# Attention and a gated feed-forward block in one kernel: copies moved between engines, weight decode moved, one pair's sums in other PSUM banks

## The chip, the cores and the metric

One core of a Trainium2 chip runs the whole program. The metric is the device time of one execution in microseconds (us), median of several runs. The engines are TensorE (PE in the profile), VectorE (DVE), ScalarE (ACT), GpSimd (POOL) and SyncE (SP), whose queue issues nearly all DMAs.

## The reference

Attention over 4 batches, 8 heads, 576 positions and 64 channels, with a bias that a small two-layer network makes from the distance of two positions, and then a feed-forward block over the 2304 tokens of 512 channels with 2048 hidden units. All data is fp32.

```python
scores = scale * q @ k.T + bias.transpose(2, 0, 1)[None]
attn = np.exp(scores - np.max(scores, axis=-1, keepdims=True))
attn = attn / (np.sum(attn, axis=-1, keepdims=True) + 1e-09)
x = (attn @ v).transpose(0, 2, 1, 3).reshape(B * S, H * D)
h = x @ w_in
r = np.maximum(h, 0.0)
out = (s * (r * r) + b) @ w_out
```

The weights `w_in` and `w_out` arrive as 64-bit floats, so the kernel loads them as pairs of 32-bit words and puts the fp32 bits together itself ("decode").

## The kernel before, in words

**Stages.** First the bias table is made and stored (about the first 48 us). Then come 16 pairs (a head and two batches), numbered p = 0 to 15. Last comes the feed-forward part, whose first products begin while the last pair ends.

**A pair** has five steps, u = 0 to 4. Step number n = 5p + u issues, in this order: the transposes of the probabilities of unit n on TensorE (`probs_t`, line 349, into the two PSUM tiles named `tps`), the score products of unit n + 2 (`scores`, lines 275 and 282, into `sps`), and the sums over values of the pair before (`av`, lines 438 and 441, into `xps`). VectorE adds the bias to `sps` and takes the row's least value (`biased`, line 297, DVE's custom instruction, writes `tt` and `mn`). ScalarE makes the exponentials (`expo`, line 308, `pr`). The transposed probabilities leave the two `tps` tiles by two copies: the first half on ScalarE (line 377), the second on VectorE (line 379), both into `pt`. There are only two `tps` tiles, so the transposes of the next step wait for both copies. At u = 3 VectorE makes the reciprocal row sums (`norm`, lines 320 and 322), and at u = 4 both engines make four small copies (lines 393 and 395). `tails` (line 398) is one more ScalarE copy at u = 2. When a pair's sums are complete VectorE multiplies them by the reciprocals (lines 444 and 445) into `rb`. The sums lie in one PSUM tile, `xps`, of which there is one buffer.

**Decode in the pairs.** A generator (`early_work`) spreads the decode of the first group of weights over the pairs 1 to 12: eight blocks, each with one step on ScalarE (line 494, absolute value), one on GpSimd (line 496), and three on VectorE (lines 498, 501, 504).

**Feed-forward.** Weights and tokens are cut in 2 x 2 blocks and multiplied by a seven-product scheme: each item n (a group of 512 hidden units and 768 tokens, 12 items) has two halves s, and each half seven products m (`product`, line 638, into `hps`). The operands of a product are sums of blocks (lines 544 and 588), split into a high part (ScalarE, line 597, `x_hi`) and the rest (VectorE, line 601, `x_lo`). The results are combined (lines 660 to 719) into `gt`, and multiplied by `w_out` (`project`, line 754, into `o`).

**What sets the order.** The order of each engine's queue is the order in which the program is written. In the feed-forward part it is a table of slots: slot T issues one product, some projections, and then the events that `at(T, ...)` put there, sorted by a small priority. Slots 0 to 13 hold a product alone, slot 14 six projections and a product; the later slots hold one product each and in every seven slots twelve projections.

**Where the stages meet.** After the last pair's transposes the program runs `prep` for seven operands of the first tokens, two products, starts the decode of two blocks of the second group of `w_in` (`soon_w`, raw tiles `rw`), makes two sums, issues the last `av` of pair 15, and only then the combining of slot 1, whose first step (`keep`, line 660) copies the first product's bank.

```python
for m in FIRST:
    prep(m)
product(0, 0, FIRST[0], False)
product(0, 0, FIRST[1], False)
decs = [decode_w(*e) for e in soon_w]
```

Of the kernel before, what the change touches and what calls it, by code (L numbers as in the profile page):

```python
# [26 lines left out]
def attention_moe(ctx, tc, q, k, v, w_in, w_out, dist, par, out):  # L27
# [310 lines left out]
    def probs_t(n):  # L338
# [79 lines left out]
    late_x = []  # L418
# [6 lines left out]
    def av(p, i, hf):  # L425
# [4 lines left out]
        if i == 0 and hf == 0:  # L430
            accs[p] = ps_x.tile([128, 2, 512], F32, tag="x", name="xps")
        ps = accs[p]
        n = END if hf else CUT
        c = slice(hf * CUT, hf * CUT + n)
        for x in range(2):
            o = ps[64 * x:64 * x + 64, hf, 0:n]
            if kb < 4:
                nc.tensor.matmul(o, vt[:, 4 * x + kb, :], pt[:, kb, x, c], start=(i == 0), stop=(i == 4))  # L438
            else:
                d = slice(64 * (x ^ hf), 64 * (x ^ hf) + 64)  # L440
                nc.tensor.matmul(o, vt[d, 8 + x, :], ptr[d, c], start=False, stop=False)
        if i == 4 and hf == 1:
            xs = rbs.pop(p)
            nc.vector.tensor_tensor(xs[:, 0:CUT], ps[:, 0, 0:CUT], xs[:, 0:CUT], op=ALU.mult)
            nc.vector.tensor_tensor(xs[:, CUT:S], ps[:, 1, 0:n], xs[:, CUT:S], op=ALU.mult)
# [7 lines left out]
    soon_w = []  # L453
# [34 lines left out]
    def decode_w(kind, g, i):  # L488
# [17 lines left out]
        r = w_raw.pop((kind, g, i))  # L506
        if (kind, g, i) not in soon_w:
            free_raw.append(r)
# [483 lines left out]
    def x_make(q, m, free):  # L992
        x_new(q, m)
        for e in range(2):
            x_hi(q, m, e)
        for e in range(2):
# [9 lines left out]
    free_raw[:] = [op.tile([128, 1536], U32, tag="q", name=f"rw{i}", bufs=2)[:, 0:1024] for i in range(2)]  # L1006
    soon_w.extend((0, 1, i) for i in range(2))
    for e in soon_w:
        load_w(*e)
# [10 lines left out]
    for m in FIRST:  # L1020
        prep(m)
# [43 lines left out]
    at(18, lambda: free_raw.extend(raws))  # L1065
# [6 lines left out]
    def fresh_x(q, free, slots):  # L1072
        for o, e in slots:
# [3 lines left out]
            if not isinstance(e, str):  # L1077
                at(o, lambda e=e: x_make(q, e, free))
# [3 lines left out]
    def fresh_w(g):  # L1082
        base = 42 * (g - 1)
        first = g == 1
        if first:
            passes = 6 * [0] + [32, 32, 32, 32, 34, 34]
# [5 lines left out]
        for kind in range(2):  # L1092
            for i in range(4):
                if (kind, g, i) in soon_w:
                    continue
# [6 lines left out]
                at(t0 - 6, lambda e=(kind, g, i): load_w(*e))  # L1102
# [8 lines left out]
        for name, o in (("S1", 35), ("S2", 35), ("S3", 38), ("S4", 40)):  # L1111
            at(base + o, lambda name=name: w_sum(name, nc.vector), 1)
# [10 lines left out]
    fresh_x(2, sums2, ((19, "T1"), (19, 1), (20, "T2"), (21, 6), (25, 5), (25, "T3"), (25, 7), (27, 2), (27, "T4"), (28, 3),  # L1123
                       (28, 4)))
# [92 lines left out]
```

## Time and profile before

| what | us |
|---|---|
| median of 3 runs | 644.83 (644.72 to 645.71) |
| the profiled execution | 646.3 |
| its span in the profile | 644.5 |
| TensorE busy | 628.5 (98%), 5418 matmuls |
| VectorE busy | 509.2 (79%) |
| ScalarE busy | 449.8 (70%) |
| GpSimd busy | 161.9 (25%) |

The span is the time from the first to the last instruction that the profile shows; the execution's own time is 1.8 us more. Busy shares are averages over the three stages, so each stage has to be read by itself. Matmuls are pipelined: the busy time of TensorE is not the time at its full rate. What tells more is from which start to which start a group of matmuls goes, and at which granted clock.

### The profile page before, as it was taken

The page shows a single profiled execution, that of the slowest core. Times are in us where ns is not written, and L with a number is a line of the kernel's source. Part 1 is how long each engine was busy: PE and PEld are TensorE (multiplying, and loading weights), DVE is VectorE, ACT ScalarE, POOL GpSimd, SP SyncE. Part 2 cuts the span into 40 slices and gives each one's busy share as a digit, 9 for nine tenths or more (in the row PEclk, how much of TensorE's full clock was granted, in tenths as well). Part 3 has the DMA queues.
Part 4 walks back from the last instruction along what each step waited for, and adds up shares of the span by engine and source line. Part 5 has one row for each costly group of instructions (what it writes and reads, how often), then busy time and mean ns, then how long its engine had stood idle before and what let it go on. Part 6 is the DMA issues. An engine that isn't in the chain of part 4 may idle for free.

```text
span 644.5 us, 14517 instructions
## 1 busy us (share of the span) xinstructions
PE 628.5 (98%) x5418; PEld 509.2 (79%) x5418; DVE 509.2 (79%) x1093; ACT 449.8 (70%) x945; POOL 161.9 (25%) x196
## 2 busy tenths in 40 slices
PE   8999999999999999899999999999999999999997
PEld 5667666666666666788999999899999999999985
DVE  7988899999999988889787776687976696775542
ACT  7988888888788888597877775566575565665440
POOL 6991433445876434000000100000100000000000
PEclk9999999999999999899999999999999999999999
DMA  5987977766767665774621646302547210718112
GB/s 154 340 260 241 285 233 243 257 231 198 254 214 232 190 207 157 253 274 161 219 80 58 242 158 201 143 11 77 212 160 282 85 34 1 270 49 280 64 49 99
DMA packets 51058, 115.27 MB, mean 179 GB/s; under 512 B 10156, under 2 KB 18860, under 8 KB 50988
## 3 DMA queue, kind: packets, MB, share of 16 engines
q1 hardware_dynamic: 50652, 114.08, 52.6%
q8 instruction: 43, 0.70, 0.5%
q10 hardware_dynamic: 208, 0.26, 0.1%
q14 instruction: 27, 0.22, 0.1%
q0 software_dynamic: 128, 0.00, 0.0%
HBM read 83.59 MB, written 30.14 MB: 176 GB/s over the span
## 4 chain that ended last, share of the span: by engine, by line
PE 77%; DVE 8%; DMA 5%; ACT 5%; issue 3%; SPq 1%; POOL 1%; DVEq 0%; ACTq 0%
PE o L754 29%; PE hps L638 25%; PE bps L168 6%; PE sps L275 6%; PE xps L438 5%; PE tps L349 4%; ACT pr L308 3%; DVE tt L297 2%; DMA kt<-in_k_dram 1%; DVE pt L379 1%; DVE x L601 1%; DMA rw<-in_moe_w_in_dram 1%; DMA wd<-xt 1%; ACT pt L377 1%; DMA big<-in_moe_w_out_dram 1%
## 5 line engine op out<-in xcount | busy, mean ns | idle before, releaser
L754 PE MATMUL o<-wo,gt 128*128 128x512 f32 x864 | 205.2, 391 | 0.1
L638 PE MATMUL hps<-x,wi 128*128 128x384 f32 x1008 | 185.3, 338 | 3.0 <-ACT h L660 2.3
L754 PEld LDWEIGHTS o<-wo,gt 128*128 128x128 f32 x864 | 161.4, 188 | 32.5 <-DVE gt L719 0.6
L638 PEld LDWEIGHTS hps<-x,wi 128*128 128x128 f32 x1008 | 178.5, 189 | 7.9 <-ACT h L660 2.9
L308 ACT ACTIVATE pr<-tt,mn 128x576 f32<-128x576 f32 x144 | 110.7, 770 | 34.6 <-DVE mn L297 34.0
L297 DVE CUSTOM_DVE_ANT_0 tt<-sps,bt 128x576 f32<-128x576 f32 x128 | 91.4, 751 | 8.8 <-PE sps L275 7.4
L349 PEld LDWEIGHTS tps<-ident,pr 64*128 64x128 f32 x1216 | 44.4, 137 | 42.4 <-issue 17.2
L438 PE MATMUL xps<-pt,vt 128*64 128x256 f32 (+1 forms) x512 | 76.0, 418 | 1.5 <-PE xps L438 1.0
L275 PE MATMUL sps<-kr,qr 64*128 64x288 f32 x768 | 72.8, 307 | 1.0 <-DVE mn L297 0.7
L702 ACT ACTIVATE h<-h,sb 128x384 f32<-128x384 f32 x72 | 50.8, 706 | 18.3 <-DVE h L698 17.2
L683 ACT ACTIVATE h<-hps 128x384 f32<-128x384 f32 x24 | 11.7, 489 | 74.2 <-PE hps L638 74.2
L275 PEld LDWEIGHTS sps<-kr,qr 64*128 64x128 f32 x768 | 58.3, 186 | 2.4 <-DVE mn L297 2.2
L349 PE MATMUL tps<-ident,pr 64*128 64x64 f32 x1216 | 56.1, 229 | 3.6 <-ACT pt L377 1.4
L687 DVE SCALAR_TENSOR_TENSOR h<-h,sb 128x384 f32<-128x384 f32 x24 | 14.8, 617 | 44.7 <-ACT h L683 44.3
L379 DVE COPY pt<-tps 128x512 f32<-128x512 f32 x64 | 43.9, 685 | 7.7 <-PE tps L349 7.3
L438 PEld LDWEIGHTS xps<-pt,vt 128*64 128x64 f32 x512 | 31.4, 136 | 21.8 <-issue 9.3
L496 POOL TENSOR_SCALAR wf<-wf 128x512 f32<-128x512 f32 x16 | 11.6, 729 | 143.1 <-ACT wf L494 142.9
L719 DVE TENSOR_TENSOR gt<-h,gt 128x384 fp32r<-128x384 f32 x72 | 39.5, 551 | 4.8 <-ACT gt L710 4.7
L168 PE MATMUL bps<-f,pt__125 128*32 128x79 f32 (+46 forms) x640 | 40.3, 402 | 1.3 <-ACT stg L172 0.6
L710 ACT ACTIVATE gt<-h 128x384 fp32r<-128x384 f32 x72 | 37.8, 526 | 2.3
L135 DVE TENSOR_SCALAR f<-lg,thr 128x432 f32<-128x432 f32 (+9 forms) x68 | 39.2, 652 | 0.0
L168 PEld LDWEIGHTS bps<-f,pt__125 128*32 128x32 f32 x640 | 23.9, 113 | 17.8 <-issue 6.8
(148 smaller groups left out, 841.5 us busy)
## 6 DMA issues: line engine op xcount, KB each, us to landing
x<-xs SPq DMA_DIRECT2D x24, 768.0 KB
bias<-stg SPq DMA_DIRECT2D x36, 295.5 KB
xs<-x SPq DMA_DIRECT2D x12, 768.0 KB
bt<-bias SPq DMA_DIRECT2D x7, 1152.0 KB
kt<-in_k_dram SPq DMA_DIRECT2D x16, 464.0 KB
wd<-in_moe_w_out_dram SPq DMA_DIRECT2D x12, 512.0 KB
x<-xt SPq DMA_DIRECT2D x28, 192.0 KB
qt<-in_q_dram SPq DMA_DIRECT2D x16, 320.0 KB
```

The lines of the kernel that those rows point to most:

```text
L135: nc.vector.tensor_scalar(o, lg[:, 0:nb, 0:16], thr[:, col], None, op0=ALU.max)
L168: nc.tensor.matmul(pb[32 * c:32 * c + 32, base + a:base + b], w2bd, mov, start=True, stop=True)
L275: nc.tensor.matmul(o, a, b, start=(i == 0), stop=(i == 2))
L297: nc.vector.tensor_tensor_reduce(tt.rearrange("p (a b) -> p a b", a=2), ps[x][:, :, 0:HALF], bias.rearrange("p (a b) -> p a b", a=2), -1.0 ...
L308: nc.scalar.activation(pr[:, x], tts.pop((n, x)), AF.Exp, bias=mn[:, x:x + 1], scale=-1.0, accum_out=sums[p][:, col // 3, col % 3:col % 3 ...
L349: nc.tensor.matmul(outs[r], src[d], ident[d, d], is_transpose=True, start=start, stop=True, skip_group_check=not start)
L379: nc.vector.tensor_copy(o, i)
L438: nc.tensor.matmul(o, vt[:, 4 * x + kb, :], pt[:, kb, x, c], start=(i == 0), stop=(i == 4))
L638: nc.tensor.matmul(ps, w_ops[m][:, w, k, s], xo[p, m][:, x, k], start=(first and i == 0), stop=(i == 5), skip_group_check=not first)
L702: return lambda: nc.scalar.activation(tmp[fo, j], tmp[fo, j], AF.Identity, bias=b_, scale=s_)
L719: nc.vector.tensor_tensor(lo, tmp[fo, j], hi, op=ALU.subtract)
L754: nc.tensor.matmul(os_t[t], gt[:, a, tok], w[:, b], start=(begin and i == 0), stop=(fo == 3 and i == 2))
```

## The change

1. In the pairs 1 to 13, at the odd units (t = 1 and 3 of five), both copies of transposed probabilities are made by ScalarE.
2. The sums of the last pair (15) go to two tiles of the transposes' pool (`aps`, tag "t") in place of the single `xps` buffer; the last step of pair 15 is issued after four products in place of two.
3. `soon_w` is gone. All four blocks of the second group's `w_in` are loaded into the buffer `wd` and decoded in the slots 25, 28, 32 and 35, the three VectorE steps of a block together. Five operands are prepared before the first two products and two behind them.
4. The two halves of each operand of the second and third 768 tokens are issued one slot apart: the high parts (ScalarE) at slot o - 1, the rest (VectorE) at slot o. Some of the slots o are others than before.

```diff
-                if r == 0:
+                if r == 0 or (t % 2 and 0 < p < 14):
                     nc.scalar.activation(o, i, AF.Copy)
                 else:
                     nc.vector.tensor_copy(o, i)
...
-            accs[p] = ps_x.tile([128, 2, 512], F32, tag="x", name="xps")
-        ps = accs[p]
+            if p < NP - 1:
+                ps = ps_x.tile([128, 2, 512], F32, tag="x", name="xps")
+                accs[p], halves[p] = ps, (ps[:, 0], ps[:, 1])
+            else:
+                halves[p] = [ps_t.tile([128, 512], F32, tag="t", name="aps") for _ in range(2)]
+        ps = halves[p]
...
-    for m in FIRST:
+    for m in FIRST[:5]:
         prep(m)
...
-    decs = [decode_w(*e) for e in soon_w]
-    for d in decs:
-        next(d)
-    for d in decs:
-        next(d)
     x_sum(1, "T1", 0, nc.vector, sums1)
     x_sum(1, "T1", 1, nc.vector, sums1)
-    next(att)
-    store_xt(NP - 1)
-    copy_x()
-    for k in range(6):
-        at(k + 1, lambda d=decs[k // 3]: next(d))
     fire(1)
+    for m in FIRST[5:]:
+        prep(m)
     product(0, 0, FIRST[2], False)
     fire(2)
     product(0, 0, FIRST[3], False)
     fire(3)
+    next(att)
+    store_xt(NP - 1)
+    copy_x()
...
-                at(o, lambda e=e: x_make(q, e, free))
+                at(o - 1, lambda e=e: x_begin(q, e))
+                at(o, lambda e=e: x_end(q, e, free))
...
-            passes = 6 * [0] + [32, 32, 32, 32, 34, 34]
+            passes = [25, 25, 25, 28, 28, 28, 32, 32, 32, 35, 35, 35]
...
-    fresh_x(1, sums1, ((12, 1), (12, "T2"), (13, 6), (14, 5), (14, "T3"), (15, 7), (16, 2), (16, "T4"), (17, 3), (18, 4)))
+    fresh_x(1, sums1, ((12, 1), (12, "T2"), (14, 6), (14, 5), (14, "T3"), (16, 7), (16, 2), (16, "T4"), (18, 3), (18, 4)))
```

How this moves instructions is seen in the queues. First VectorE in pair 3, where `wf` is a weight block in decode and `sps`, `bt` the scores and their bias. Before:

```order
L498 TENSOR_SCALAR wf<-wf 128x512
L379 COPY pt<-tps 128x8x64
L297 ISA tt,mn<-sps,bt 128x576
L297 ISA mn 128x1
L297 ISA tt,mn<-sps,bt 128x576
L297 ISA mn 128x1
L501 SCALAR_TENSOR_TENSOR wf<-big,wf 128x512
L379 COPY pt<-tps 128x8x64
```

Now:

```order
L501 TENSOR_SCALAR wf<-wf 128x512
L297 ISA tt,mn<-sps,bt 128x576
L297 ISA mn 128x1
L297 ISA tt,mn<-sps,bt 128x576
L297 ISA mn 128x1
L504 SCALAR_TENSOR_TENSOR wf<-big,wf 128x512
L379 COPY pt<-tps 128x8x64
```

The copy of the odd unit behind the first decode step has left VectorE's queue (line numbers grow by 3); on ScalarE the same place now holds two rows of line 377 one behind the other.

Second, ScalarE where the stages meet: `x` are operands of products, `rw` raw weights, `h` the first result. Before:

```order
L597 ACTIVATE x_5188<-big 128x384 x2
L597 ACTIVATE x_5189<-ws_1026 128x384
L597 ACTIVATE x_5189<-h_5274 128x384
L494 ACTIVATE wf<-rw_5269 128x512
L494 ACTIVATE wf<-rw_5270 128x512
L660 ACTIVATE h_5274<-hps 128x384
L683 ACTIVATE h_5275<-hps 128x384
```

Now:

```order
L661 ACTIVATE h_5270<-hps 128x384
L598 ACTIVATE x_5188<-big 128x384 x2
L598 ACTIVATE x_5189<-ws_1026 128x384
L598 ACTIVATE x_5189<-h_5270 128x384
L684 ACTIVATE h_5271<-hps 128x384
```

The two decode steps have gone from ahead of `keep` (line 660, now 661), and `keep` stands ahead of the last two operands.

Third, TensorE at the same place. Before:

```order
L638 MATMUL hps<-x_5183,wi_1008 128x384 x6
L638 MATMUL hps<-x_5184,wi_1009 128x384 x6
L438 MATMUL xps<-pt,vt 64x256 x2
L438 MATMUL xps<-pt,vt 64x320 x2
L638 MATMUL hps<-x_5185,wi_1012 128x384 x6
```

Now:

```order
L639 MATMUL hps<-x_5183,wi_1008 128x384 x6
L639 MATMUL hps<-x_5184,wi_1009 128x384 x6
L639 MATMUL hps<-x_5185,wi_1012 128x384 x6
L639 MATMUL hps<-x_5186,wi_1010 128x384 x6
L442 MATMUL aps<-pt,vt 64x256 x2
L442 MATMUL aps<-pt,vt 64x320 x2
```

The last sums of pair 15 go behind the fourth product and into `aps`.

## Rows read from the trace of the kernel before

**Rows 1.** The chain that ended last, feed-forward part: start, us, what.
```profile
312.59 4.18 PE hps L638 x24
316.77 4.12 PE o L754 x18
```

**Rows 2.** Windows: length, busy PE, PEld, DVE, ACT, POOL, clock, DMA share, GB/s.
```profile
73.72:230.31 156.59, 153.25 (x2161) 103.75 (x2160) 144.48 (x384) 130.45 (x334) 83.63 (x84) 1.00 0.70 229
86.98:100.88 13.90, 12.95 (x181) 8.73 (x180) 13.37 (x35) 10.98 (x30) 5.03 (x5) 1.00 0.80 259
230.31:242.96 12.65, 12.55 (x181) 8.54 (x180) 10.89 (x31) 10.49 (x29) 4.45 (x4) 1.00 0.67 204
```

**Rows 3.** Timeline of VectorE in pair 3 (bracket: idle before, releaser).
```profile
91.16 1.74 DVE L498 TENSOR_SCALAR wf<-wf 128x512 uint32<-128x512 uint32 x1
92.83 0.68 DVE L379 COPY pt<-tps 128x512 f32<-128x512 f32 x1
```

**Rows 4.** Timeline of TensorE in pair 3.
```profile
96.38 0.71 PE L349 MATMUL tps<-ident,pr 64*128 64x64 f32 x16 [0.86 <-ACT pt L377]
```

**Rows 5.** Groups of lines in 74 to 243: count, busy, mean ns, idle before.
```profile
L379 DVE COPY pt<-tps 128x512 f32<-128x512 f32 x52 | 35.6, 684 | 4.7 <-PE tps L349 4.5
...
L308 ACT ACTIVATE pr<-tt,mn 128x576 f32<-128x576 f32 x117 | 90.0, 770 | 27.9 <-DVE mn L297 27.3 <-ACT ptr L393 0.3
L377 ACT ACTIVATE pt<-tps 128x512 f32<-128x512 f32 x52 | 30.0, 576 | 0.0
```

**Rows 6.** Timeline of ScalarE, an odd unit, and a copy with a decode step behind.
```profile
157.61 0.57 ACT L377 ACTIVATE pt<-tps 128x512 f32<-128x512 f32 x1
158.81 0.78 ACT L308 ACTIVATE pr<-tt,mn 128x576 f32<-128x576 f32 x1 [0.63 <-DVE mn L297]
...
162.09 0.58 ACT L377 ACTIVATE pt<-tps 128x512 f32<-128x512 f32 x1
162.57 0.67 ACT L494 ACTIVATE ws<-big 128x512 f32<-128x512 f32 x1
```

**Rows 7.** Timeline of TensorE, the transposes after that odd unit.
```profile
158.92 0.71 PE L349 MATMUL tps<-ident,pr 64*128 64x64 f32 x16
```

**Rows 8.** Timeline of TensorE where the stages meet.
```profile
255.98 2.16 PE L438 MATMUL xps<-pt,vt 128*64 128x256 f32 x16 [0.97 <-PE xps L438]
...
259.89 2.37 PE L638 MATMUL hps<-x,wi 128*128 128x384 f32 x12
...
265.71 14.32 PE L638 MATMUL hps<-x,wi 128*128 128x384 f32 x72 [2.32 <-ACT h L660]
279.87 4.28 PE L754 MATMUL o<-wo,gt 128*128 128x512 f32 x18
...
299.89 1.31 PE L638 MATMUL hps<-x,wi 128*128 128x384 f32 x6 [0.68 <-DVE h L679]
```

**Rows 9.** Timeline of ScalarE where the stages meet.
```profile
264.61 0.66 ACT L494 ACTIVATE wf<-rw 128x512 f32<-128x512 f32 x1 [1.17 <-DMA rw<-in_moe_w_in_dram]
265.18 0.48 ACT L660 ACTIVATE h<-hps 128x384 f32<-128x384 f32 x1
```

**Rows 10.** Windows there (columns as in rows 2).
```profile
255.01:301.04 46.03, 41.92 (x227) 36.77 (x227) 40.43 (x83) 34.48 (x73) 1.23 (x2) 0.96 0.66 236
...
266.00:268.00 2.00, 2.00 (x8) 2.00 (x8) 1.83 (x5) 0.22 (x1) 0.00 (x0) 0.53 0.22 50
```

**Rows 11.** Timeline of VectorE: last use of the bank before slot 14's end, and a decode step.
```profile
268.84 0.69 DVE L504 SCALAR_TENSOR_TENSOR wf<-rw,wf 128x512 uint32<-128x512 uint32 x1
...
283.85 0.55 DVE L679 TENSOR_TENSOR h<-hps,h 128x384 f32<-128x384 f32 x1
```

**Rows 12.** Windows, a later stretch of the feed-forward part.
```profile
306.14:370.59 64.45, 64.45 (x326) 58.50 (x325) 48.93 (x89) 47.88 (x93) 5.60 (x8) 1.00 0.42 150
```

**Rows 13.** Waits in 254.9 to 301.1: us in total, times, longest.
```profile
DVE rb L444 <- DMA rb<-rs: 2.2, 1, 2.2
...
DVE x L601 <- ACT x L597: 1.3, 2, 0.8
```

More of the change, by code (lines that the diff above doesn't have):

```diff
@@ L416, in direct_x @@
             late_x.append((x_in(0)[r, KB - 1, S:2 * CH], xs[64:128, 0:2 * CH - S]))
-    late_x = []
+    late_x, halves = [], {}
     def copy_x():
@@ L435, in av @@
         for x in range(2):
-            o = ps[64 * x:64 * x + 64, hf, 0:n]
+            o = ps[hf][64 * x:64 * x + 64, 0:n]
             if kb < 4:
@@ L443, in av @@
             xs = rbs.pop(p)
-            nc.vector.tensor_tensor(xs[:, 0:CUT], ps[:, 0, 0:CUT], xs[:, 0:CUT], op=ALU.mult)
-            nc.vector.tensor_tensor(xs[:, CUT:S], ps[:, 1, 0:n], xs[:, CUT:S], op=ALU.mult)
+            nc.vector.tensor_tensor(xs[:, 0:CUT], ps[0][:, 0:CUT], xs[:, 0:CUT], op=ALU.mult)
+            nc.vector.tensor_tensor(xs[:, CUT:S], ps[1][:, 0:n], xs[:, CUT:S], op=ALU.mult)
             xts[p] = xs
@@ L452, in attention_moe @@
     highest = bits_as_float(0x47EFFE00)
-    soon_w = []
     sources = (w_in.bitcast(U32), w_out.bitcast(U32))
@@ L505, in decode_w @@
             bits, raw[:, :, 0], 29, bits, op0=ALU.logical_shift_right, op1=ALU.bitwise_or)
-        r = w_raw.pop((kind, g, i))
-        if (kind, g, i) not in soon_w:
-            free_raw.append(r)
+        free_raw.append(w_raw.pop((kind, g, i)))
         yield
@@ L990, in prep, with x_begin @@
             x_lo(0, m, e, x_free[e])
-    def x_make(q, m, free):
+    def x_begin(q, m):
         x_new(q, m)
@@ L995, in x_make, with x_end @@
             x_hi(q, m, e)
+    def x_end(q, m, free):
         for e in range(2):
@@ L1005, in attention_moe @@
     free_x.append(op.tile([128, 2, 2, CH], F32R, name="x7"))
[L1006 to L1009, printed above, removed]
     for i in range(3):
@@ L1064, in attention_moe @@
     raws = [mix["wd"][:, i] for i in range(3)]
-    at(18, lambda: free_raw.extend(raws))
+    at(18, lambda: free_raw.__setitem__(slice(None), raws))
     for n in range(1, NI + 1):
@@ L1093, in fresh_w @@
             for i in range(4):
-                if (kind, g, i) in soon_w:
-                    continue
                 k, (t0, t1, t2) = 4 * kind + i, passes[12 * kind + 3 * i:12 * kind + 3 * i + 3]
@@ L1100, in begin @@
                     next(decs[k])
-                at(t0 - 6, lambda e=(kind, g, i): load_w(*e))
+                at(t0 - (4 if (kind, g, i) == (0, 1, 3) else 6), lambda e=(kind, g, i): load_w(*e))
                 at(t0 - 2, begin)
@@ L1111, in fresh_w @@
         for name, o in (("S1", 35), ("S2", 35), ("S3", 38), ("S4", 40)):
-            at(base + o, lambda name=name: w_sum(name, nc.vector), 1)
+            at(base + o, lambda name=name: w_sum(name, nc.vector))
         for i, m in enumerate(ORDER):
@@ L1119, in attention_moe @@
             at(4 + i // 2, lambda m=m: store_x(0, m), 1)
-    fresh_x(1, sums1, ((12, 1), (12, "T2"), (13, 6), (14, 5), (14, "T3"), (15, 7), (16, 2), (16, "T4"), (17, 3), (18, 4)))
+    fresh_x(1, sums1, ((12, 1), (12, "T2"), (14, 6), (14, 5), (14, "T3"), (16, 7), (16, 2), (16, "T4"), (18, 3), (18, 4)))
     for a in range(KB):
         at(6, lambda a=a: load_x(2, a))
-    fresh_x(2, sums2, ((19, "T1"), (19, 1), (20, "T2"), (21, 6), (25, 5), (25, "T3"), (25, 7), (27, 2), (27, "T4"), (28, 3),
-                       (28, 4)))
+    fresh_x(2, sums2, ((18, "T1"), (19, 1), (21, "T2"), (23, 6), (25, 5), (25, "T3"), (27, 7), (28, 2), (28, "T4"), (30, 3), (30, 4)))
     for g in range(1, NG):
```

## The prediction

> **What bounds the kernel now.** I read the chain of waits first. From 301 us to the end it is TensorE alone, products and projections in turn, 24 matmuls in 4.18 us and 18 in 4.12 us [rows 1], so 0.1742 us for a product's matmul and 0.2289 us for a projection's. A later window shows TensorE busy for all of its 64.45 us at the full clock [rows 12]. Nothing in the change alters a matmul, so this stage can't get shorter; what is to be won lies where TensorE waits, in the pairs and where the stages meet.
>
> Second, the windows, one for each pair. Twelve pairs (2 to 13) take 156.59 us; the next, in which no decode is left, takes 12.65 [rows 2]. So the twelve lose 156.59 - 12 x 12.65 = 4.79 us. The worst, pair 3, takes 13.90 us, and VectorE is busy in 13.37 of them, against 10.89 in the pair without decode [rows 2]. There one decode step took 1.74 us and the copy of the odd unit came behind it [rows 3]; the scores that follow came late, the exponentials after them, and TensorE's transposes waited 0.86 us [rows 4]. In these pairs TensorE and VectorE bound the period together.
>
> Third, the timelines where the stages meet. From 255.01 us (the start of TensorE's first long wait) to 301.04 takes 46.03 us [rows 10]. The work in it at full rate: four steps of the last pair's sums from 255.98 to 259.89, 3.91 us [rows 8], and a fifth of about 1.1; 150 matmuls of products, 26.13; 36 of projections, 8.24; together 39.4. Lost are 6.6 us. [...] (a) 0.97 us: the last pair's sums wait for the only `xps` buffer [rows 8]. (b) 2.32 us: the third product waits for `keep` [rows 8], because `keep` stands on ScalarE behind two decode steps whose raw weights were still on their way [rows 9]. [...] The rest, 1.7 us, is scattered; 0.68 of it is a product that waits for a PSUM bank which VectorE had not emptied [rows 8], and VectorE did its last work on the bank before slot 14 only at 283.85 [rows 11], four microseconds after TensorE had gone on.
>
> **The change part by part.**
>
> *Copies to ScalarE.* 13 pairs x 2 = 26 copies leave VectorE. They cost 0.684 us each there and 0.576 on ScalarE [rows 5]. VectorE loses 17.8 us of work, 1.37 in a pair, which is more than the 0.40 that an average pair loses. On ScalarE the place is free: in an odd unit it waits 0.63 us for VectorE behind its copy [rows 6], and over 13 pairs 27.3 us in all [rows 5]. A following ScalarE instruction starts 0.48 us behind a copy's start [rows 6]; the second copy would end at 157.61 + 0.48 + 0.57 = 158.66, and the next transposes begin at 158.92 [rows 7]. So it fits with 0.26 us to spare, and 0.15 of the idle time is left. In the 8 pairs in which a decode step of ScalarE stands near (0.67 us, [rows 6]) the fit is broken: 0.58 of pitch less 0.15 and 0.26 leaves some 0.15 us late. I keep that in all eight, 1.2 us, though VectorE may hide it. Gain: 4.79 - 1.2 = 3.6 us. Bounds: nothing, if ScalarE takes the place of VectorE as the bound, and 6.0, if the 0.1 us that even the pair of 12.65 us shows as idle TensorE [rows 2] goes in all twelve.
>
> [...]
>
> *Other banks for the last pair.* Removes (a), 0.97 us: the two `tps` tiles are free when the small copies of the last transposes end, and these stand in VectorE's queue ahead of the multiplication that now frees `xps`. Bounds 0 and 0.97; I take all.
>
> *Decode out of the way.* ScalarE meets `keep` with nothing slow ahead of it: (b), 2.32 us. With no such wait the clock has no cause to fall: (c), 1.62 us. What is late next? The two products put ahead of the last sums give TensorE about 2.1 us more work, longer than `keep` needs. The multiplication behind the last sums waits for the reciprocals, 2.2 us in the kernel before [rows 13]; their load was behind the two weight loads in SP's queue, which are gone, and TensorE needs what stands behind it on VectorE only some five products later. The six VectorE steps (at most 0.69 us each [rows 11], 4.1 in all) go to slots 25 to 35, together with two more blocks that were at 32 and 34; there VectorE is idle for 64.45 - 48.93 = 15.5 us of 64 [rows 12]. I cost them at nothing; without that cover they would cost up to 4.1.
>
> *Halves one slot apart, slots moved.* VectorE's waits for ScalarE's halves (1.3 us [rows 13]) go, and with the 4.1 us above VectorE is no longer four microseconds late at slot 14. TensorE's share is the rest of 1.7 us. I take half, 0.8: some operands are ready one slot later than before, so a few short waits may stay. Bounds 0 and 1.7.
>
> **Sum.** 3.6 + 0.97 + 2.32 + 1.62 + 0.8 = 9.3 us. The profiled execution took 646.3 us, with a span of 644.5; the span should become 635.2 and such an execution 637.0. The median of the runs stands 1.5 below that execution: 644.83 - 9.3 = **635.5 us**.
>
> **The rivals.**
>
> *ScalarE becomes the bound of the pairs.* It was busy in 10.98 us of pair 3 and gets 1.0 to 1.15 more, in a period of 12.65 [rows 2]. For it: in the pairs with decode only half a microsecond is left, and the exponentials stand behind the copies. Against it: the idle 27.3 us sit just behind those copies. Gain of the pairs then 0: 644.83 - 5.7 = 639.1 us.
>
> *A new wait where the stages meet.* The loads, the multiplication or the stores of operands hold a queue, and a wait as long as (b) stays. The clock then falls as now: (b), (c) and the 0.8 are not won, and 644.83 - 3.6 - 0.97 = 640.3 us. The rows show the fall once, behind a wait of 2.32 us. [...]
>
> *Slower: the two copies hold the transposes.* Where both `tps` tiles now empty one after the other, TensorE can lose what used to run on two engines at once. The place is the odd unit; if the exponentials there start late by all of the 0.26 us, each second copy shows, and 0.57 - 0.26 = 0.31 us, 26 times, is 8.1 lost, with the pairs' gain gone too: 644.83 + 8.1 - 5.7 = 647.2 us. It becomes slower than before from 5.7 / 26 = 0.22 us a copy on. Against it speaks that ScalarE waits there in every pair without decode.
>
> **How the numbers follow.** My forecast has a chance of 0.74, ScalarE as the bound 0.11, a new wait 0.09, the slower case 0.06. From no change the measurement can tell about 0.2%, 1.3 us. The first three cases are all faster by more: 0.93 with a little taken off for mishaps of both kinds; same 0.02; slower 0.05. The range: below, everything gained, 6.0 + 6.6 = 12.6, is hardly all to be had, so 632.6; above, the first rival's 639.1 and a little of the second, 639.4.
>
> **What would show it.** In the pairs: windows of 12.6 to 12.8 us where 13.0 to 13.9 stood, VectorE near 11 and ScalarE near 12 us busy in them, no idle ScalarE behind the copies of the odd units. Where the stages meet: no wait of TensorE ahead of the last pair's sums, none for `keep`, a granted clock of 1.00 throughout, slot 14 some 5 us earlier relative to the last pair, and no wait on a PSUM bank at slot 24. Later: product and projection groups of 4.18 and 4.12 us as now. Wrong would be: transposes waiting for ScalarE's copy in every odd unit; a granted clock below 1 around the first products; idle TensorE between slots 25 and 35.

## The result, and the profile after

| kernel | median of its runs, us | runs of before beside them, us | ratio, 95% interval |
|---|---|---|---|
| changed kernel | 639.67 (638.14 to 640.51, 6 runs) | 645.82 (6 runs) | 0.990 [0.988, 0.992] |

The change gains about 6.2 us; 9.3 were forecast. By the ratio, 644.83 becomes 638.4 us, 2.9 above the forecast of 635.5. The sign and the range hold, the size does not.

I cut the span of the profiled execution into four stretches: from the first short scores (line 282, matmuls of 64x64, one group in each pair) to those of pair 2; from there to those of the last pair; from there to the 18 projections of slot 24 (301.04 us in the kernel before); and the rest. The windows of before, cut so:

```profile
54.97:81.62 26.65, 24.93 (x348) 17.99 (x345) 21.73 (x60) 22.16 (x58) 11.10 (x13) 1.00 0.90 282
81.62:250.14 168.52, 165.60 (x2345) 112.06 (x2341) 155.39 (x414) 140.36 (x359) 86.35 (x86) 1.00 0.69 223
250.14:301.04 50.90, 46.69 (x293) 39.28 (x289) 43.67 (x93) 38.56 (x85) 5.20 (x6) 0.97 0.64 224
301.04:644.50 343.46, 339.33 (x1687) 304.95 (x1686) 239.75 (x432) 202.07 (x376) 15.82 (x22) 1.00 0.37 133
```

and of after. In both the columns are the stretch, its length, and the busy time of each engine, then the granted clock, the DMA share and GB/s:

```profile
55.11:82.93 27.82, 25.29 (x347) 17.99 (x345) 19.90 (x57) 23.16 (x59) 10.82 (x13) 1.00 0.88 271
82.93:249.70 166.77, 164.20 (x2345) 111.26 (x2341) 141.90 (x391) 150.91 (x384) 86.11 (x86) 1.00 0.70 225
249.70:294.50 44.80, 44.62 (x291) 37.60 (x289) 40.12 (x87) 37.32 (x83) 3.97 (x4) 1.00 0.74 255
294.50:637.80 343.30, 339.34 (x1687) 305.00 (x1686) 242.95 (x439) 203.05 (x377) 17.42 (x24) 1.00 0.38 133
```

So the 6.7 us by which the span is shorter (644.5 to 637.8) are made of: first pairs 1.17 lost, later pairs 1.75 won, meeting of the stages 6.10 won, the rest nothing. For the later pairs and the meeting I had forecast 3.6 and 5.7. **Where the stages meet** the timeline of TensorE after shows what rows 8 showed before (start, length, line, operands, count, and in brackets an idle time ahead):

```profile
254.47 2.16 PE L442 MATMUL aps<-pt,vt 128*64 128x256 f32 x16
256.56 0.77 PE L445 MATMUL aps<-ptr,vt 64*64 64x256 f32 x8
257.26 1.19 PE L442 MATMUL aps<-pt,vt 128*64 128x256 f32 x8
258.38 4.43 PE L639 MATMUL hps<-x,wi 128*128 128x384 f32 x24
...
263.87 11.00 PE L639 MATMUL hps<-x,wi 128*128 128x384 f32 x60
274.70 4.28 PE L755 MATMUL o<-wo,gt 128*128 128x512 f32 x18
...
288.24 6.43 PE L639 MATMUL hps<-x,wi 128*128 128x384 f32 x36
294.50 1.78 PE L755 MATMUL o<-wo,gt 128*128 128x512 f32 x7
```

No row has a bracket. The last pair's sums (now `aps`) follow at once; four products (24 matmuls) and, behind the last sums, sixty more matmuls run without a wait for `keep`, and these 60 take 10.83 us against 60 x 0.1742 = 10.45. The granted clock is 1.00 where 0.53 stood [rows 10].

**In the pairs** the groups of lines in 74 to 243 us answer to rows 5 (count, busy, mean ns, idle time ahead):

```profile
L308 ACT ACTIVATE pr<-tt,mn 128x576 f32<-128x576 f32 x119 | 91.5, 770 | 17.1 <-DVE mn L297 15.4
...
L377 ACT ACTIVATE pt<-tps 128x512 f32<-128x512 f32 x76 | 41.6, 578 | 0.0
L349 PEld LDWEIGHTS tps<-ident,pr 64*128 64x128 f32 x988 | 35.6, 137 | 35.1 <-ACT pt L377 21.4 <-issue 7.4 <-ACT ptr L393 6.4
...
L379 DVE COPY pt<-tps 128x512 f32<-128x512 f32 x28 | 19.1, 683 | 2.1 <-PE tps L349 2.1
```

A copy takes what it took on either engine (0.578 and 0.683 us; 0.576 and 0.684 before [rows 5]). 24 of them in this window have changed sides, and ScalarE's idle time ahead of the exponentials falls from 27.9 to 17.1 us, 0.45 a copy: the room was there. TensorE's loads for the transposes, though, now wait 21.4 us of their time for ScalarE's copy, where the same view of before has 11.2.

What pairs 2 to 14 lose is no longer spread. I took the start of each pair's short scores from the timeline; the differences, in us:

| from the short scores of pair | 0 | 1 | 2 | 3 | 4 | 5 | 6 | 7 | 8 | 9 | 10 | 11 | 12 | 13 | 14 |
|---|---|---|---|---|---|---|---|---|---|---|---|---|---|---|---|
| before | 13.22 | 13.43 | 12.64 | 13.80 | 13.19 | 12.71 | 12.64 | 13.02 | 13.20 | 13.62 | 12.65 | 13.01 | 12.72 | 12.66 | 12.66 |
| after | 13.30 | 14.52 | 12.94 | 13.01 | 12.60 | 12.59 | 13.01 | 13.01 | 12.72 | 13.01 | 13.02 | 13.01 | 12.60 | 12.59 | 12.66 |

Seven pairs stand at 13.0 us, 0.42 above the best. In six of them a ScalarE decode step (line 497 after) lies in unit 1 (pairs 2, 6, 10) or in unit 2 (pairs 3, 7, 11); in pairs 4 and 8 it lies in unit 3, and they take 12.60 and 12.72. The seventh, pair 9, has none: there a VectorE decode step took 1.56 us (174.39) beside two of GpSimd's instructions (174.38 to 177.09), and such steps come up again below. Pair 10, with the step in unit 1, in ScalarE's timeline:

```profile
183.82 1.05 ACT L377 ACTIVATE pt<-tps 128x512 f32<-128x512 f32 x2
184.77 0.69 ACT L497 ACTIVATE ws<-big 128x512 f32<-128x512 f32 x1
185.36 0.76 ACT L308 ACTIVATE pr<-tt,mn 128x576 f32<-128x576 f32 x1
...
186.88 0.57 ACT L377 ACTIVATE pt<-tps 128x512 f32<-128x512 f32 x1
```

and TensorE's:

```profile
187.51 0.71 PE L349 MATMUL tps<-ident,pr 64*128 64x64 f32 x16 [0.43 <-ACT pt L377]
```

The two copies of the odd unit go first, in 1.05 us; the decode step behind them pushes the exponentials back by 0.59 (184.77 to 185.36), and so the single copy of the next unit (186.88), and the transposes wait 0.43 us for it.

With the step in unit 2 the way is another, and it is older than the change. Pair 7, first in the kernel before, then in the changed one: the timelines of ScalarE (exponentials behind the decode step), of VectorE (the reciprocal row sums `ru` made from them) and, in the changed kernel, of TensorE (the score products behind these):

```profile
148.77 0.76 ACT L308 ACTIVATE pr<-tt,mn 128x576 f32<-128x576 f32 x1
...
149.65 0.17 DVE L320 TENSOR_SCALAR ru<-su 128x9 f32<-128x9 f32 x1
```

```profile
148.28 0.67 ACT L497 ACTIVATE ws<-big 128x512 f32<-128x512 f32 x1
...
149.23 0.77 ACT L308 ACTIVATE pr<-tt,mn 128x576 f32<-128x576 f32 x1
...
150.12 0.16 DVE L320 TENSOR_SCALAR ru<-su 128x9 f32<-128x9 f32 x1 [0.72 <-ACT pr L308]
...
151.50 0.38 PE L275 MATMUL sps<-kr,qr 64*128 64x288 f32 x1
151.94 1.05 PE L275 MATMUL sps<-kr,qr 64*128 64x288 f32 x11
```

Counted from the pair's short scores (146.60 and 147.08), the exponentials start at 2.17 us before and at 2.15 after, the row sums at 3.05 and 3.04, and the pair takes 13.02 and 13.01. In pair 5 of the changed kernel, which has no such step, they start at 1.69 and 2.60. VectorE, now free of its copy, waits 0.72 us for the exponentials, its bias products come late, and TensorE, whose loads wait 0.27 us for them, goes on with the second score matmul (151.94) just when the second of these (151.12, 0.75 us long) has emptied a score bank. The copies neither brought this loss nor could take it away.

### The profile page after: what moved, and what is told of

It is laid out like the page before. It is cut to its first block, busy times and chain, and to the rows that moved or that the text cites. A ratio compares the mean times of both kernels' runs of the same rounds, so it can differ in the third digit from the quotient of the medians.

```text
span 637.8 us, 14517 instructions
## 1 busy us (share of the span) xinstructions
PE 624.7 (98%) x5418; PEld 506.8 (79%) x5418; DVE 493.5 (77%) x1067; ACT 461.5 (72%) x971; POOL 161.6 (25%) x196
## 4 chain that ended last, share of the span: by engine, by line
PE 82%; DMA 6%; ACT 5%; DVE 3%; issue 2%; SPq 1%; POOL 1%; DVEq 0%; ACTq 0%
PE o L755 31%; PE hps L639 28%; PE sps L275 6%; PE bps L168 6%; PE xps L442 6%; PE tps L349 4%; ACT pr L308 4%; DMA vt<-in_v_dram 2%; ACT pt L377 1%; DVE tt L297 1%; DMA big<-in_moe_w_in_dram 1%; DMA kt<-in_k_dram 1%; PE aps L442 1%; DVE f L135 1%; DMA be<-btail 1%
## 5 line engine op out<-in xcount | busy, mean ns | idle before, releaser
L442 PE MATMUL xps<-pt,vt 128*64 128x256 f32 x480 | 71.5, 419 | 0.0
L377 ACT ACTIVATE pt<-tps 128x512 f32<-128x512 f32 x90 | 49.4, 578 | 0.0
L442 PEld LDWEIGHTS xps<-pt,vt 128*64 128x64 f32 x480 | 29.2, 136 | 18.3 <-issue 9.0
L168 PE MATMUL bps<-f,pt__125 128*32 128x79 f32 (+44 forms) x640 | 39.7, 390 | 2.1 <-POOL f L137 0.7
```

The lines of the kernel that those rows point to most:

```text
L168: nc.tensor.matmul(pb[32 * c:32 * c + 32, base + a:base + b], w2bd, mov, start=True, stop=True)
```

## The experiments

Twelve runs were made, one of them of the changed kernel again. "Meeting" in this table is the stretch from the last short scores to the 18 projections of slot 24, "first" and "pairs" are the two stretches ahead of it, all of the profiled execution; the other columns are medians of runs beside runs of before. A profile is one execution and can lie off its kernel's median: that of only banks took 648.89 us, that of only copies 642.69, that of no ScalarE step 638.15.

| kernel | median | less than before, ratio | first | pairs | meeting |
|---|---|---|---|---|---|
| before | 644.83 | | 26.65 | 168.52 | 50.90 |
| changed | 639.67 | 6.2, 0.990 [0.988, 0.992] | 27.82 | 166.77 | 44.80 |
| changed, again | 639.55 | 6.3, 0.989 [0.986, 0.992] | 26.76 | 168.01 | 44.86 |
| only copies | 644.24 | 2.3, 0.996 [0.993, 0.999] | 27.29 | 166.32 | 48.99 |
| no copies | 641.67 | 4.9, 0.992 [0.989, 0.995] | 27.66 | 169.73 | 44.82 |
| only decode | 643.14 | 3.4, 0.995 [0.991, 0.998] | 27.04 | 167.41 | 46.95 |
| only banks | 646.90 | -1.1, 1.000 [0.997, 1.002] | 26.98 | 169.32 | 52.31 |
| no halves | 640.96 | 5.6, 0.990 [0.983, 0.996] | 26.45 | 167.10 | 46.11 |
| bias first | 644.11 | 2.4, 0.996 [0.994, 0.999] | 34.79 | 166.84 | 44.81 |
| three steps a block | 641.75 | 4.8, 0.992 [0.989, 0.994] | 27.32 | 168.78 | 44.81 |
| both | 644.73 | 1.8, 0.997 [0.994, 0.999] | 32.71 | 167.57 | 44.82 |
| ScalarE's step moved | 638.62 | 7.2, 0.988 [0.985, 0.990] | 26.46 | 167.85 | 44.82 |
| the same, values later | 638.36 | 7.5, 0.988 [0.984, 0.991] | 27.31 | 166.99 | 44.81 |
| no ScalarE step | 636.66 | 9.3, 0.986 [0.984, 0.988] | 26.73 | 166.30 | 44.81 |

My theory from the profile of the changed kernel: the meeting of the stages went as forecast, the place of ScalarE's decode step cost the pairs what was missing, and pair 1's loss was a late transfer. The rival: the copies themselves brought pair 1's wait, and VectorE's decode steps hold the pairs.

**Only the copies** (label only_copies), on the kernel before:

```diff
-                if r == 0:
+                if r == 0 or (t % 2 and 0 < p < 14):
                     nc.scalar.activation(o, i, AF.Copy)
```

> The kernel before with one edit of the change: the second copies of 26 transposes on ScalarE. Theory A (the pairs gain what they gained in the whole change, and the wait of pair 1 came by a late transfer): pairs 2 to 13 take about 154.3 us where 156.6 stood, pair 1 stays near 12.5, the kernel is about 2.3 us faster (643.5). Theory B (the wait of 1.6 us in pair 1 comes with the copies): pair 1 takes about 14.1 and the kernel is only some 0.6 us faster (645.2). Both: the excess over 12.6 us stands in pairs 2, 3, 6, 7, 10, 11, each about 0.43. Nothing changes where the stages meet (46.0 us). My forecast had 3.6 us for it.

**All but the copies** (no_copies), the same line put back in the changed kernel:

> The changed kernel without the copies on ScalarE. Where the stages meet it should take about 40.0 us where 46.0 stood, so some 6.0 us less than before (639.8); pairs 2 to 13 take 156.6 us as before. Theory A (pair 1's wait is a late transfer, free of the copies): the wait may be there or not, whatever the copies do. Theory B (it comes with the copies): pair 1 takes about 12.5 us, no wait of VectorE on its bias product.

The pairs took 166.32 us with the copies alone and 169.73 without them. One profile is not enough here: over four profiles without the copies (before, only decode, only banks, no copies) the pairs take 167.41 to 169.73, mean 168.7, and over five with them and the old places of the decode (changed twice, only copies, no halves, bias first) 166.32 to 168.01, mean 167.0. The two ranges touch, but the copies are worth about 1.7 us of the 3.6 forecast, and nothing where the stages meet (44.82 and 44.80); the runs agree (4.9 without them, 6.2 or 6.3 with them). The 13.0 us of the six pairs (12.92 to 13.17) stood in all five profiles with the copies, as both theories expected. The four without them tell the six apart: pairs 2, 6 and 10 took 12.53 to 12.75 us in ten of twelve cases, so there the copies brought the loss; pairs 3, 7 and 11 took 13.01 to 13.80 already.

Pair 1's wait does not hang on the copies: no copies had it (14.34 us), while the changed kernel run again had 13.52, no halves 13.22 and only copies 12.58 (but 14.71 in pair 0). The rival falls on this point. What only copies won beyond its pairs came where the stages meet, unforeseen: `keep` was 1.38 us late instead of 2.32. TensorE's timeline of that kernel:

```profile
263.21 3.40 PE L638 MATMUL hps<-x,wi 128*128 128x384 f32 x18 [1.38 <-ACT h L660]
266.97 1.32 PE L638 MATMUL hps<-x,wi 128*128 128x384 f32 x6 [0.36 <-DVE h L669]
```

ScalarE's second decode step there, which the raw weights release after a wait of 1.18 us, stood at 262.11, 2.50 us earlier than before [rows 9], while the last sums had begun only 1.55 us earlier (254.43 for 255.98). So the transfer did not keep the pace of the pairs; why, was not followed. The granted clock stayed at 1.00 (windows of the same kernel, the clock ahead of the last two columns):

```profile
263.20:265.20 2.00, 1.99 (x11) 1.99 (x12) 2.00 (x5) 0.49 (x1) 0.27 (x1) 1.00 0.08 20
265.20:267.20 2.00, 1.64 (x10) 1.31 (x9) 2.00 (x6) 0.62 (x1) 0.00 (x0) 1.00 0.98 274
```

**Only the decode moved** (only_decode), on the kernel before:

```diff
-    soon_w.extend((0, 1, i) for i in range(2))
-    for e in soon_w:
-        load_w(*e)
...
-            passes = 6 * [0] + [32, 32, 32, 32, 34, 34]
+            passes = [25, 25, 25, 28, 28, 28, 32, 32, 32, 35, 35, 35]
...
```

> The kernel before with the decode of the second group's first two blocks moved behind the meeting of the stages, with the bunches, and nothing else: same banks for the last pair, same order of products, halves of operands in one slot. My steps (b) and (c): no wait of TensorE for keep, a granted clock of 1.0 there, 3.9 us less. Step (a), 0.97 us before the last pair's sums, stays. Rival: keep still waits behind other work and the clock still falls: under 1.5 us less. A second rival: without the two products ahead, the last sums' multiplication comes late, and a wait on PSUM takes 1 to 2 us of it back.

TensorE's timeline of that kernel:

```profile
255.27 2.16 PE L438 MATMUL xps<-pt,vt 128*64 128x256 f32 x16 [0.97 <-PE xps L438]
...
262.61 12.78 PE L635 MATMUL hps<-x,wi 128*128 128x384 f32 x72
275.23 4.28 PE L751 MATMUL o<-wo,gt 128*128 128x512 f32 x18
...
295.22 1.32 PE L635 MATMUL hps<-x,wi 128*128 128x384 f32 x6 [0.69 <-DVE h L676]
```

The wait for `keep` is gone, 72 matmuls of products run from 262.61 to 275.23, 12.62 us where 14.16 stood [rows 8], and the stretch is 3.95 us shorter; steps (b) and (c) had 3.94. The 0.97 us of step (a) stays (255.27), and so does a wait of 0.69 us for a bank that VectorE has not emptied (295.22). The last sums' multiplication did not come late: the second rival of the expectation falls.

**Only the banks** (only_banks), on the kernel before:

```diff
...
+            if p < NP - 1:
+                ps = ps_x.tile([128, 2, 512], F32, tag="x", name="xps")
+                accs[p], halves[p] = ps, (ps[:, 0], ps[:, 1])
+            else:
+                halves[p] = [ps_t.tile([128, 512], F32, tag="t", name="aps") for _ in range(2)]
...
```

> The kernel before with the last pair's sums in other banks, and nothing else. My step (a) by itself: no wait of TensorE before these sums, 0.97 us less where the stages meet. Rival: the wait for keep behind it, which ends with the raw weights' transfer, grows by what was won: no gain, 2.3 + 1.0 us of wait for keep, and as much fall of the clock as before. In that case (a) counts only because the decode was moved in the same change.

TensorE's timeline of that kernel, then ScalarE's, then the windows behind the wait:

```profile
256.01 2.16 PE L442 MATMUL aps<-pt,vt 128*64 128x256 f32 x16
...
267.01 15.22 PE L642 MATMUL hps<-x,wi 128*128 128x384 f32 x70 [3.61 <-ACT h L664]
```

```profile
264.25 0.66 ACT L498 ACTIVATE wf<-rw 128x512 f32<-128x512 f32 x1 [2.49 <-DMA rw<-in_moe_w_in_dram]
265.92 0.66 ACT L498 ACTIVATE wf<-rw 128x512 f32<-128x512 f32 x1 [1.01 <-DMA rw<-in_moe_w_in_dram]
```

```profile
267.00:269.00 2.00, 1.99 (x6) 2.00 (x7) 1.84 (x5) 0.00 (x0) 0.28 (x1) 0.50 0.22 50
269.00:271.00 2.00, 2.00 (x7) 2.00 (x7) 1.09 (x2) 0.92 (x2) 0.00 (x0) 0.50 0.96 295
271.00:273.00 2.00, 2.00 (x8) 2.00 (x8) 1.03 (x3) 0.18 (x1) 0.00 (x0) 0.50 0.99 399
```

The wait of 0.97 us went, and the wait for `keep` grew from 2.32 to 3.61 us, since it ends with the raw weights' transfer (ScalarE's steps at 264.25 and 265.92). The granted clock then stood at 0.50 for 6 us (267 to 273); the 72 matmuls behind the wait took 15.40 us (267.01 to 282.41) where 14.16 stood [rows 8], and the stretch was 1.4 us longer than before. The runs tell no difference (1.000). The rival was right: (a) counts only because the same change took the decode away.

**Halves in one slot again** (no_halves), on the changed kernel:

```diff
-                at(o - 1, lambda e=e: x_begin(q, e))
+                at(o, lambda e=e: x_begin(q, e))
                 at(o, lambda e=e: x_end(q, e, free))
```

with the slots of the operands as before.

> The changed kernel with both halves of an operand in one slot and the slots as before. My step for the halves is inside the 0.8 us for the scattered rest: theory A, 0.5 to 1.0 us slower than the changed kernel, with waits of VectorE for ScalarE's half of the operand and a short wait of TensorE on a PSUM bank or an operand. Theory B, VectorE has room there anyway: within 0.3 us of the changed kernel, VectorE's waits for ScalarE's half are back and cost nothing.

TensorE's timeline of that kernel has the wait of before again:

```profile
293.73 1.31 PE L639 MATMUL hps<-x,wi 128*128 128x384 f32 x6 [0.65 <-DVE h L680]
```

The meeting took 46.11 us, 1.31 more than with the halves apart, 0.65 of it in the wait for a bank at slot 24 (293.73; 0.68 before [rows 8]). Theory A, and more than its upper end; the four runs (638.52 to 643.35 us) are too few to tell it. With (a), 0.97, that is 2.28, against the 2.15 by which the changed kernel is shorter there than only decode.

**The bias of pair 2 first** (bt_first), on the changed kernel:

```diff
+        if n == 2:
+            load_bias(2, 0, 4)
         if u == 2 and cur:
             load_q(p + 2)
             load_k(p + 2)
...
         if n == 2:
-            load_bias(2, 0, 4)
             load_v(1)
```

> The changed kernel with the bias of pair 2 issued on SP's queue ahead of the queries and keys of that pair. Theory A (VectorE's 1.55 us wait in pair 1 is for that bias): the wait goes, pair 1 takes about 12.5 us where 14.16 stood, the kernel is about 1.6 us faster than the changed one (638.0). Theory B (TensorE's or ScalarE's work is late there): pair 1 stays at 14.1, no difference. Theory C (the queries or keys are late instead): a wait of the same size moves to TensorE's scores of pair 2, no difference.

In the changed kernel VectorE's wait in pair 1 (timeline of VectorE, 70 to 76 us) stood at 72.97, although the scores that it reads were issued at 70.28 and were 1.04 us long; what was left to wait for is the bias tile `bt`, whatever the bracket names. This is inferred: no row shows when the bias landed.

```profile
72.97 0.76 DVE L297 CUSTOM_DVE_ANT_0 tt<-sps,bt 128x576 f32<-128x576 f32 x1 [1.55 <-PE tps L349]
```

With the bias ahead in SP's queue it was theory C, and worse than a draw. GpSimd's timeline of that kernel, and of the changed one:

```profile
72.14 0.61 POOL L247 TENSOR_SCALAR qr<-qt 128x512 fp32r<-128x512 f32 x1 [7.96 <-DMA qt<-in_q_dram]
```

```profile
65.97 0.62 POOL L247 TENSOR_SCALAR qr<-qt 128x512 fp32r<-128x512 f32 x1 [1.87 <-DMA qt<-in_q_dram]
```

The queries, issued some 2.4 us later than before, arrived 6.2 us later; TensorE waited 4.29 and 1.01 us for the keys that GpSimd made behind them, the granted clock was 0.50 in the windows from 74 to 81 us, and the first two pairs took 34.79 us. The share of the DMA engines at that time was 0.99 and 0.95 in the changed kernel:

```profile
56.00:62.00 6.00, 5.10 (x62) 4.45 (x62) 4.91 (x16) 5.05 (x14) 0.18 (x1) 1.00 0.99 326
62.00:68.00 6.00, 5.83 (x86) 4.11 (x86) 4.10 (x10) 5.21 (x14) 4.04 (x7) 1.00 0.95 323
```

At the 326 GB/s of the first row the 1152 KB of bias now ahead of the queries take some 3.6 us, an estimate; with the 2.4 that makes 6.0 of the 6.2. So neither of the two orders tried is free. This fits theory A's cause (the wait is for transfers) and refutes the cure.

**Three steps a block** (abs_u3): the generator of the first group's decode is written so that a block takes the three steps of one pair, with ScalarE's step always in unit 3:

```diff
-        for _ in range(3):
+        for _ in range(5):
             yield
...
         soon.append(lambda: begin(0))
         yield
-        yield
         next(ahead[0])
...
             if j > 4:
+                wout_hi(0, i - 1, nc.gpsimd)
                 wout_lo(0, i - 1, nc.gpsimd)
...
-            yield
-            if kind == 1:
-                wout_hi(0, i, nc.gpsimd)
-            elif i == 3:
+            if kind == 0 and i == 3:
...
```

> The changed kernel with the decode of the first group set at three steps a block and pair, so that ScalarE's decode step always stands in unit 3 of a pair. Theory A (the place of ScalarE's decode step, in unit 1 or 2, costs 0.43 us in each of six pairs): all of pairs 2 to 13 take 12.6 to 12.7 us, in all 151.8 where 154.3 stood, 2.5 us faster than the changed kernel. Theory B (ScalarE is loaded up to the period whatever the place): the pairs with a decode step still take about 13.0, no gain, or a loss as the steps of VectorE then stand in more pairs. The bias of pair 2 is as in the changed kernel, so pair 1 may still wait.

Pairs 1 to 3 took 12.59, 12.60 and 12.61 us, with a ScalarE step in unit 3 of pairs 2 and 3: for these theory A holds. Pairs 4, 6 and 7 took 13.57, 14.07 and 14.01. The timelines of VectorE and of GpSimd in pairs 4 and 6:

```profile
107.83 0.43 DVE L501 TENSOR_SCALAR wf<-wf 128x512 uint32<-128x512 uint32 x1 [0.44 <-POOL wf L499]
...
109.44 1.57 DVE L504 SCALAR_TENSOR_TENSOR wf<-big,wf 128x512 uint32<-128x512 uint32 x1
...
148.14 1.69 DVE L501 TENSOR_SCALAR ws<-ws 128x512 uint32<-128x512 uint32 x1
```

```profile
148.00 1.54 POOL L248 TENSOR_TENSOR kr<-kt,kr 128x640 fp32r<-128x640 f32 x1
```

VectorE's first decode step now waits for GpSimd's (107.83); in pair 6 it lies beside GpSimd's making of the keys and takes 1.69 us where 0.43 is its time alone. The second takes 1.57 where it is 0.69. The row at 148.14 ends at 149.83, 0.29 behind the end of GpSimd's instruction (149.54), and in pair 3 of the kernel before the row of 1.74 us [rows 3] ends at 92.90, 0.27 behind the end of this one:

```profile
91.06 1.57 POOL L248 TENSOR_TENSOR kr<-kt,kr 128x640 fp32r<-128x640 f32 x1
```

From these two cases I infer that VectorE's step stood still for most of GpSimd's instruction; no row names such a wait, and another step took no longer beside GpSimd than alone (0.69 at 148.24 before, where GpSimd's row starts at 148.58). The cure of one term made the other worse.

**Both** (abs_u3_bt):

> Both of the last two edits on the changed kernel. If they act on different pairs, the gains add: 1.6 + 2.5 = 4.1 us faster than the changed kernel, near 635.5. If one wait hid the other: the larger alone, 2.5 us.

Neither end: the first pairs took 32.71 us, nearly as long as with the bias first, and pairs 2 to 4 and 10 to 13 stood at 12.6, the others at 12.92 to 14.02.

**The changed kernel again, and ScalarE's step moved alone** (after_again, abs_moved):

> The changed kernel once more, on the chip of the next runs. Theory A (pair 1's loss is a race of transfers that no edit touches, since it came in kernels with and without the copies): the span from the first short scores to those of pair 2 lies anywhere between 26.4 and 27.8 us, pairs 2 to 13 take about 154 us again. Theory B: pair 1 takes 14.2 us again, as it would if the change itself caused it. The six excesses of about 0.43 us in pairs 2, 3, 6, 7, 10, 11 should stand again.

> The changed kernel with five of ScalarE's decode steps, those of pairs 3, 6, 7, 10 and 11, put into unit 3 of a pair (the one of pair 2 stays in unit 1) and GpSimd's step after three of them one slot later; VectorE's decode steps stay where they are. Theory A (its place costs 0.43 us each): five pairs of 13.0 us become 12.6, some 2.1 us less between pair 2 and 14 (152.2 where 154.3 stood), 2 us faster than the changed kernel on the same chip. Theory B (VectorE's decode steps beside GpSimd make the excess, as they made 13.6 to 14.1 us in single pairs of the kernel with three steps a block): no gain, the pairs stay at 13.0.

```diff
+            r = (1 + j) % 3
             next(ahead[j])
+            if r == 0:
+                soon.append(lambda j=j: begin(j + 1))
...
             next(ahead[j])
-            soon.append(lambda j=j: begin(j + 1))
+            if r == 2:
+                soon.append(lambda j=j: begin(j + 1))
             yield
             next(ahead[j])
-            if j + 1 < len(early):
+            if r == 1:
+                soon.append(lambda j=j: begin(j + 1))
+            elif j + 1 < len(early):
                 next(ahead[j + 1])
...
```

The changed kernel took 26.76 us in the first pairs, as theory A of this run has it. It showed the six pairs at 12.97 to 13.11 us again, and three others, free of a ScalarE step in units 1 and 2, at 13.09, 13.22 and 13.06 (pairs 4, 5, 13), so that its later pairs took 168.01 us. With the step moved, pairs 3, 6 and 7 took 12.69, 12.62 and 12.65, as theory A says; pairs 4, 10 and 11 took 13.73, 13.47 and 13.59, as theory B says, behind VectorE steps like this one, just ahead of the short scores of pair 4:

```profile
106.83 1.76 DVE L501 TENSOR_SCALAR wf<-wf 128x512 uint32<-128x512 uint32 x1
```

With no GpSimd instruction beside it such a step takes 0.42 us (123.06 in the changed kernel). On the same chip this kernel is 0.9 us faster than the changed one (638.62 and 639.55), with intervals that overlap; theory A had 2.

**The values of pair 2 later** (abs_moved_v), on the last kernel:

```diff
                 load_be(p + 1)
-                load_v(p + 1)
+                if p > 1:
+                    load_v(p + 1)
...
+        if n == 9:
+            load_v(2)
```

> The kernel abs_moved, with the values of pair 2 (320 KB) loaded four steps later, out of the stretch in which pair 1 waits for the bias. Theory A (the first pairs wait for transfers, in sum): up to 1 us less in pair 1, never more than 26.5 us from the first short scores to those of pair 2, and that much faster than abs_moved. Theory B (the order in the queue, not the sum, decides): no difference beyond the spread of the runs.

Theory B: 27.31 us in the first pairs of its profile, 638.36 us in the runs, no difference from 638.62 that they can tell.

**No ScalarE step** (no_abs), on the changed kernel. It leaves out the absolute value, so its weights are not those of the reference; it serves to time the pairs without that step:

```diff
-        nc.scalar.activation(full, raw[:, :, 1].bitcast(F32), AF.Abs)
         yield
-        nc.gpsimd.tensor_scalar(full, full, highest, lowest, op0=ALU.min, op1=ALU.max)
+        nc.gpsimd.tensor_scalar(full, raw[:, :, 1].bitcast(F32), lowest, highest, op0=ALU.max, op1=ALU.min)
```

> The changed kernel without ScalarE's decode steps: GpSimd's step reads the raw weights itself, and the absolute value is left out, so negative weights are decoded to the smallest magnitude. Theory A (ScalarE's step is what holds pairs 2, 3, 6, 7, 10 and 11 at 13.0 us): these six take 12.6 to 12.7, pairs 2 to 13 some 2.5 us less than in the changed kernel, unless a VectorE decode step beside GpSimd's work lies long in one of them. Theory B (VectorE's decode steps hold them): single pairs of 13.0 to 13.9 stay, as many as in the kernel abs_moved, and the gain over the changed kernel is under 1 us. Where the stages meet nothing changes (44.8 us from the last short scores).

The six pairs took 12.49, 12.62, 12.92, 12.64, 12.64 and 12.81 us, together 1.9 less than in the changed kernel, and the median is 3.0 lower than the changed kernel's 639.67. Pairs 4, 5 and 8 took 13.35, 13.12 and 13.27; VectorE's decode steps at 106.54, 117.15, 121.72 and 158.57 took 1.45, 1.13, 1.13 and 1.40 us, so the long steps stay, and took back most of the 1.9 in this profile (pairs 2 to 13: 153.65 us, 154.11 in the changed kernel). Both theories are right, each for its pairs.

## Why the prediction was right, and where its sum was off

**Where the stages meet: right, term by term.** (a) 0.97 was taken whole, and the row of after shows no wait; alone it gave nothing, which the step did not say. (b) and (c), 2.32 + 1.62 = 3.94: only decode gave 3.95. The 1.62 are what the 72 matmuls behind the wait took, 14.16 us [rows 8], less 72 x 0.1742 = 12.54, with a granted clock of 0.53 from 266 to 268 us [rows 10]; only decode ran 72 in 12.62, and after the change the clock is 1.00. The halves and the scattered rest (6.6 - 0.97 - 2.32 - 1.62 = 1.7), 0.8 between 0 and 1.7: no halves shows 1.31, so half was too little. The six VectorE steps costed at nothing: TensorE's products have 0.1 us of idle time in the whole program after the change (a group of the page; its 336 ns is the mean length of records that overlap, from start to start it is 0.1742 us [rows 1]), so their cover held:

```profile
L639 PE MATMUL hps<-x,wi 128*128 128x384 f32 x1008 | 183.7, 336 | 0.1
```

In all, 5.71 us were forecast and 6.10 measured.

**The pairs: the mechanism right, a term mis-sized.** The step starts from 4.79 us as if all of it were VectorE's lateness and would go with 1.37 us of work less in a pair, and takes off 1.2: "0.58 of pitch less 0.15 and 0.26 leaves some 0.15 us late. I keep that in all eight". The 1.2 came out by luck, from two errors. The 0.26 was the room between the second copy of an odd unit and the transposes behind it [rows 6, 7]. A decode step of ScalarE in unit 1 lies behind both copies, though, and makes the next unit's single copy late, which has no such room (in pair 5 of the changed kernel it ends at 122.78 and the transposes begin at 122.84): 0.58 less 0.15 is 0.43, and 0.43 is what the row shows (187.51). And the copies bring this in three pairs (2, 6, 10), not in eight: 3 x 0.43 = 1.3 us.

What is missing lies in the 4.79, the term that was too large. In pairs 3, 7 and 11 ScalarE's step in unit 2 holds the row sums after the change as before; with 0.42 above the best in each, 1.3 us of the 4.79 was nothing that a lighter VectorE could win. The other part: the 1.74 us of VectorE's decode step [rows 3] were read as work, where the same step alone takes 0.42 and the long one lay beside GpSimd's making of the keys (91.06). A lighter VectorE did not end that: the step of 1.56 us at 174.39 stood in both kernels (1.55 at 174.40 before), and pair 9 of the changed kernel took 0.42 us above the best; other executions show long steps in other pairs (1.76 at 106.83 above). 3.6 - 1.3 = 2.3 stands against the measured mean of 1.7, and the 0.6 between them is, by my estimate, of that kind.

**The first pairs** were not in the sum. They take 26.45 to 27.82 us whatever the edits but that of the bias, with DMA shares of 0.90 before and 0.88 after over the stretch, and the profiled execution of the changed kernel had one of the long ones: 1.17 lost in it, 0.11 in the other profile.

**The rivals.** ScalarE as the bound of the pairs came true in part, in six pairs out of thirteen, and by the copies in three of them. The new wait where the stages meet did not come. Nor did the slower one: ScalarE's two copies hold no transposes in the pairs of 12.6 us. The two copies of an odd unit took 1.05 us together (183.82), which is 0.48 + 0.57, so the pitch of 0.48 [rows 6] holds. Where the wait for `keep` was only shortened, to 1.38 us in only copies, the granted clock stayed at 1.00; 0.53 and 0.50 followed on the waits of 2.32 us [rows 8, 10] and 3.61 us.

**Left open.** Why the bias is late in pair 1 in one execution and not in the next was not settled; and what decides in which pairs a VectorE step takes long, beyond that it varies from one execution to the next of one kernel. What GpSimd did beside such a step is shown for the kernels before and changed and for pair 6 of three steps a block, not for the others. A kernel that takes the absolute value without ScalarE and keeps the result was not tried.

## What to carry to other kernels

Work moved to an engine "where it waits anyway" must be followed past the place where it is put: look at the next thing in that engine's queue, and count only the room that is left there. Before a lateness is priced as one engine's, look whether a second engine is late at the same place by as much. A wait that ends with a transfer can swallow what is won ahead of it (in only banks 0.97 us were won and the wait grew by 1.29); price such edits together, and don't expect a gain from one alone. And before a difference of one microsecond between two profiles is given a cause, look at the same stretch in a second execution of the same kernel.

## What the runs showed of the hardware

A VectorE shift on 128x512 words took 0.42 us with no GpSimd instruction beside it (122.83 before, 123.06 after) and 0.55 to 1.74 with one (196.11 and 91.16 before). A shift-and-or took 0.69 alone (146.83 after), 0.68 to 1.19 with one (161.20 before), and up to 2.08 in only banks (221.72), where no row shows GpSimd. The longer times count as busy time of VectorE: the 1.74 lie in the 13.37 busy us of pair 3 [rows 2]. GpSimd's own row, making the keys, took 1.54 to 1.87 before and 1.55 to 1.88 after. VectorE's bias product beside these GpSimd rows kept its 0.75 to 0.76 in both.

In bias first, with DMA shares of 1.05 and 1.00 from 70 to 77 us, 320 KB of queries that were issued some 2.4 us later, behind 1152 KB of bias, arrived 6.2 us later than in the changed kernel.
